# Pairs of batches share a tile of their last tokens, softmax sums on another engine, and a new order of work

## The chip, the cores and the metric

The kernel runs on one core of a Trainium2 chip. The core has a matrix engine (TensorE, PE in the profile, with its weight loads as PEld), a vector engine (VectorE, DVE), an engine for functions of one element (ScalarE, ACT), a programmable vector engine (GpSimd, POOL) and a sync engine (SyncE, SP), whose queue issues most transfers here. Each takes its instructions in the order in which the program lists them and waits where an instruction's input isn't ready. Matmuls write to PSUM, eight banks of 512 float32 for each of 128 partitions; everything else lies in SBUF. The metric is device time in microseconds, lower is better: the median of three runs.

## The reference, cut to what matters

Eight batches of 576 tokens, 8 heads of 64 channels. Keys and values are averaged over 8 neighbouring tokens, which leaves 72; ordinary softmax attention follows, and its output x (576 tokens by 512 channels) goes through a mixing block:

```
k_p, v_p = means of k, v over 8 tokens                  # 72 rows
attn = softmax(q @ k_p.T / 8)                           # 576 x 72 per head
x = attn @ v_p                                          # heads side by side: 576 x 512
theta = x @ w_theta
zr, zi = x * cos(theta), x * sin(theta)
y = w_tok_r @ zr + w_tok_i @ zi                         # over tokens, 576 x 576 each
u = x + y
out = u + max(u @ w_ch, 0)
```

All in float32. The three weights come as float64 and are turned into float32 pairs on the chip.

## The kernel before, in words

Products that need more than one pass's accuracy are split: a matrix a becomes a high part (`xh`, `zh`, `uh`, ...) and a remainder (`xl`, `zl`, `ul`), and a product is three matmuls, high by high, high by low, low by high.

The work is cut into streams, small generators that issue one step each time they are called. For each batch b:

- `k`, `v`, `Q`: loads (`load` L491, `queries` L580); `K`, `V`: the sums over 8 tokens (`pool` L518, `pool_sum` L476: three halving additions) and the layouts that attention needs (`keys` L560, `vals` L620).
- `S{b}.{m}` for five token tiles m (four of 128 tokens, the last of 64): scores, softmax (`soften` L680). Scores sit in PSUM tile `s`, two banks, of which there is one. For batches 0 and 1 (`SUMS_ON_ACT` = 2) ScalarE takes the maximum as its bias and does one exponential for each head, with the sum accumulated; for batches 2 to 7 VectorE subtracts the maximum, ScalarE does one exponential over all heads, and VectorE sums.
- `E`: for batches 2 to 7 the attention weights are transposed by VectorE and 16 small transfers (`turn` L840, for tiles 0 and 1, and for 2 to 4).
- `X{b}.{g}.{c}`: attention times values for one of four blocks of channels and for tokens 0 to 255 or 256 to 575 (`attend` L877). It writes x with channels on the partitions into `xT`, 640 columns wide: after 576 tokens the last 64 stand again (L906).
- `T{b}.{m}`: theta of one tile of 128 tokens (`rotate` L911): split x, 12 matmuls of 512 columns, then rounding to whole turns (L929, L931), 4 transposes of x, sine, absolute value, cosine, and the products with x, into `z`. Tile 4 holds the last 64 tokens twice; one sine gives cosines in one half and sines in the other (L957 to L963). So `z` has nine chunks of 128 rows.
- `Z{b}.{c}`: split of z for a block of channels (`take` L968). `M{b}.{c}.{hf}`: 27 matmuls with the token weights, for 256 or 320 tokens, added to x (`mix` L980), and the split of u.
- `F{b}.{c}.{hf}`: 12 matmuls with w_ch, maximum and sum (`final` L1015), a transposition by VectorE into `R`, and for each (b, c) four transfers to the output; those of the last batch go by halves, on two queues.

`h`, `w`, `W`, `c` are the streams of the weights, all within the first batches. The order is written out by hand as words in `SCHEDULE`: each word calls its stream once, and a last letter v, g or a says which engine (VectorE, GpSimd, ScalarE) does the step, where there is a choice. Each engine's queue is the order of the words:

```
for word in SCHEDULE.split():
    name, engine = (word[:-1], word[-1]) if word[-1] in "vga" else (word, None)
    now[0] = engine
    next(streams[name])
```

Of the kernel before, what the change touches and what calls it, by code (L numbers as in the profile page):

```python
# [9 lines left out]
F32 = mybir.dt.float32  # L10
# [20 lines left out]
D h1 k0.0 k0.1 K0.0 K0.1 K0.0a k0.2 w0.0 h0 K0.2 w0.0 Q0.0 w0.0v h0 w0.0g h1 h1v K0.2a K0.1v Q0.1 w0.0 K0 h2 Q0.0  # L31
h0g Q0.0v K0a K0 w1.0 Q0.2 K0a Q0.4 h0a h0 h0 Q0.1 Q0.1a h1v h0v S0.0 h0 w1.0 h1 S0.0 h0v Q0.3 h0 w1.0g h1 h2 S0.1
h2v S0.0 Q0.2 v0.0 S0.1 Q0.2v h2v h2 v0.1 Q0.4 h1g v0.2 k1.0 Q0.3 h2 w1.0v S0.0 h2v w0.1 S0.0 S0.1 h3 S0.2 Q0.4v
S0.0g Q0.3v S0.2 V0.0 w1.0 w0.0 S0.1 S0.2 S0.1 S0.0g S0.0 S0.3 w0.0v V0.1 S0.1g S0.3 S0.1g S0.0v V0.2 S0.2 S0.2 V0v
K1.0g S0.1 S0.3 V0 S0.3 S0.4 w0.1 S0.0 h1 S0.1v S0.2g S0.2g S0.0v k1.2 S0.1 S0.4 S0.1v X0.0.0 S0.3 h3 h1v X0.0.0v
S0.2 w0.1v X0.0.1 S0.4 w0.1v w0.1 h3a h2 X0.0.1v h3v S0.3v h3 w0.1 X0.0.3 w1.1 S0.3v S0.4 h3 k1.1 S0.2a w0.1v S0.4
S0.2 h3g S0.3 S0.3a S0.2a Q1.0 w2.0 h1 W0 w1.1 Q1.1 w1.1a h2v X0.0.3v S0.4g w3.0 S0.4g S0.3 h3 S0.3v h2 w2.0 W0a
X0.0.2 h3v X0.0.2v K1.1g w2.0a S0.4 S0.4a S0.4 Q1.0 S0.4v T0.0a w1.1a h3 Q1.1 w2.1 X0.2.3 w2.0a W0 w1.1 Q1.1a w1.0
W0 Q1.0a Q1.3 X0.2.3v w2.1 T0.0v w1.1 w3.1 w2.0 W0a W0 v1.0 Q1.2 w2.1a X0.2.1 K1 T0.0 w1.1v K1.2v w2.1a w1.0v w2.1
T0.0 X0.2.2 T0.0 W1 T0.1g w2.0 w2.0v T0.1v Q1.2 T0.0 T0.0 w3.0 X0.2.1v T0.0a X0.2.2v w3.0a V1.0v w3.0v X0.2.0 W1a  # L40
w2.1 Q1.3 T0.0 X0.2.0v T0.1 T0.3a W1 T0.3v w2.1g Q1.3a X0.2.3a T0.2a T0.1 W1 w3.1 w4.0 W1a w3.0 T0.0 T0.1 K1a T0.2g
w3.1v Q1.4 T0.2 T0.0 T0.2 W1 T0.1 v1.1 W2 T0.4g w3.1v T0.1 w4.0 T0.4v w3.0 w3.1 w3.0g w4.0a T0.1a T0.1 T0.2 W2v
T0.2 T0.2 W2 w4.0a T0.1 T0.3 W2 T0.2a W2a T0.1 T0.4 T0.2 w4.0 V1.1g c0 T0.3 w4.0 c0 w3.1 W2 T0.2 T0.2 w3.1g T0.4
T0.3 W3 c0g T0.4 T0.3 K1 T0.4 M0.0.0 T0.4 T0.3 W3a T0.4 T0.3a T0.3 T0.3 W3 T0.4 w4.0g c0 T0.3 c0 Q1.2a c0 Z0.0a W4
W4a c0v c1 Z0.0v W4 W4a c0a c0g W4 W4a V1g Q1.4 M0.0.0 M0.0.0 Z0.1a W4 K1v W4a c1 W4 W3 c1v W3a W3 c1 c1 M0.0.1
M0.0.0 c1 c1v Z0.1v c1a Z0.2a S1.0 c1g M0.1.1 S1.0 c2 Q1.4a Z0.2v c2 M0.0.1 c2v c2 c2 c2 k2.2 K2.2v c2v M0.1.0 S1.0
v1.2 S1.0 S1.0v S1.1 Z0.3a S1.0g S1.0 c3 M0.0.1g M0.1.0 S1.1 M0.1.1 V1.2g Z0.3v M0.2.0 V1v S1.0v c2a S1.1 S1.0 S1.0
S1.1 M0.3.0 M0.2.0 c2g S1.2 S1.0a c3 M0.2.0a V1 S1.0 c3v M0.0.0g S1.2 S1.1v M0.3.1 c3 S1.1v S1.2 c3 c3 M0.3.0
M0.0.0v S1.1 c3v M0.1.1v S1.1v S1.2 V1v V1v M0.0.1g M0.3.1 S1.1 S1.1 M0.2.1 Q2.0 S1.1a S1.1 X1.0.0 M0.1.1g c3a
S1.2v M0.3.1a S1.3 M0.2.1 c3g X1.0.0a M0.3.0a k2.0 S1.3 S1.2g S1.3 M0.3.1g M0.3.0g X1.0.1 M0.2.1g M0.2.1g S1.2  # L50
M0.1.0a X1.0.1v X1.0.2 F0.0.1 X1.0.2v K2.0v M0.2.0v X1.0.3 X1.0.3v S1.2a S1.4 M0.1.0v S1.3 T1.0a S1.2 S1.2 S1.2a
S1.3g S1.4 S1.3v F0.0.0 T1.0v F0.0.0 Q2.0 S1.2 S1.4 F0.0.1 k2.1 S1.3 S1.3a S1.4 F0.0.0 F0.0.1 T1.0 S1.3 v2.2 K2.1g
# [24 lines left out]
F2.0.1 X3.2.2v X3.2.3 T3.1v K5.2v F2.0.1 T3.1 S4.2 T3.0 S4.2 T3.0v T3.0 S4.3 T3.0 F2.0.1 S4.2g v5.0 T3.0 F2.1.1
# [53 lines left out]

EARLY, EXACT, V_ON_PE, K_ON_PE, Q_ON_PE, SUMS_ON_ACT = 2, 1, 1, 1, 2, 2


@with_exitstack
def tile_attn_moe(
# [52 lines left out]
    def pick():  # L191

        return now[0]
# [986 lines left out]
```

## Time and profile before

| | |
|---|---|
| runs | 614.71, 616.81, 618.32 us, median 616.81 |
| profiled execution: span, first to last instruction | 611.1 us; the page gives no other total for it |
| TensorE matmuls / weight loads busy | 590.0 / 548.7 us (97% / 90%) |
| VectorE, ScalarE, GpSimd busy | 475.6, 302.0, 331.4 us |
| granted TensorE clock, mean | 0.996 of full speed |
| chain that ended last | TensorE 60%, VectorE 18% of the span |

Busy time is the time in which an engine had at least one instruction under way. TensorE's matmuls overlap, so the mean of one is longer than the distance from one to the next; how fast matmuls really follow each other is read from the starts in a timeline, or from the chain.

### The profile page before, as it was taken

The numbers are of one execution on the slowest core, as the hardware profiler recorded it, in microseconds if no ns is written. First come the engines' busy times: TensorE is split into PE (matmuls) and PEld (weight loads), VectorE is DVE, ScalarE is ACT, GpSimd is POOL, SyncE is SP. The second block draws the span as 40 slices with busy tenths as digits, with TensorE's granted clock in tenths as the row PEclk, the third lists the DMA queues.
The fourth block names the chain that finished last, engine by engine and source line by source line (L and its number), as shares of the span: only waits on it lengthen the run. The fifth ranks groups of instructions, "written<-read, shape, count | busy, mean of one in ns | idle before, by whom it ended". The sixth has DMA issues, their size and how long they took to land.

```text
span 611.1 us, 11650 instructions
## 1 busy us (share of the span) xinstructions
PE 590.0 (97%) x4136; PEld 548.7 (90%) x4136; DVE 475.6 (78%) x933; ACT 302.0 (49%) x627; POOL 331.4 (54%) x492
## 2 busy tenths in 40 slices
PE   7899989998899999999999999999999999999997
PEld 6766889887799999999899999999999999998996
DVE  4999989889898978798978777898876875467425
ACT  3788858687743563236523652266334671515000
POOL 5561734356665778657867585337937644530130
PEclk9899999999999999999999999999999999999999
DMA  9978121368565646674527555624611331312115
GB/s 286 235 233 186 39 78 45 75 117 138 96 126 87 125 71 118 122 144 68 98 42 160 96 94 89 125 47 89 122 33 33 55 53 20 61 20 44 17 20 78
DMA packets 235386, 57.86 MB, mean 95 GB/s; under 512 B 223424, under 2 KB 223936, under 8 KB 235328
## 3 DMA queue, kind: packets, MB, share of 16 engines
q1 hardware_dynamic: 230464, 56.52, 46.1%
q10 hardware_dynamic: 4864, 0.59, 0.7%
q8 instruction: 33, 0.54, 0.4%
q14 instruction: 25, 0.20, 0.1%
HBM read 37.81 MB, written 9.44 MB: 77 GB/s over the span
## 4 chain that ended last, share of the span: by engine, by line
PE 60%; DVE 18%; DMA 5%; SPq 5%; POOL 4%; ACT 4%; issue 3%; DVEq 0%; POOLq 0%; ACTq 0%
PE py L996 31%; PE pf L1025 9%; PE pt L925 8%; PE pv L898 5%; PE s L707 3%; SPq L851 3%; DMA kpst<-in_k_dram 1%; DMA WTh_st<-in_moe_w_theta_dram 1%; DMA out_dram<-R 1%; PE px L935 1%; DVE xT L904 1%; SPq L587 1%; DVE zl L977 1%; DVE oT L1031 1%; DVE mx L741 1%
## 5 line engine op out<-in xcount | busy, mean ns | idle before, releaser
L996 PE MATMUL py<-WTh,zh 128*128 128x256 f32 (+1 forms) x576 | 86.7, 295 | 1.0 <-ACT zh L197 1.0
L996 PE MATMUL py<-WTh,zl 128*128 128x256 f32 (+1 forms) x576 | 87.1, 295 | 0.5 <-DVE oT L1031 0.5
L996 PE MATMUL py<-WTl,zh 128*128 128x256 f32 (+1 forms) x576 | 86.4, 293 | 0.0
L996 PEld LDWEIGHTS py<-WTh,zh 128*128 128x128 f32 x576 | 79.9, 188 | 1.6 <-ACT zh L197 1.4
L996 PEld LDWEIGHTS py<-WTh,zl 128*128 128x128 f32 x576 | 79.0, 188 | 1.0 <-DVE oT L1031 0.7
L996 PEld LDWEIGHTS py<-WTl,zh 128*128 128x128 f32 x576 | 79.7, 187 | 0.0
L1002 DVE TENSOR_TENSOR xT<-py,xT 128x256 f32<-128x256 f32 (+1 forms) x64 | 28.6, 447 | 41.4 <-PE py L996 41.3
L182 POOL TENSOR_TENSOR en<-e_eps,ri 128x256 f32<-128x256 f32 (+3 forms) x63 | 30.6, 505 | 42.9 <-DVE ri L766 32.6
L929 ACT ACTIVATE g<-pt,c_magic 128x512 f32<-128x512 f32 x38 | 26.1, 687 | 48.1 <-PE pt L925 28.1
L1025 PE MATMUL pf<-uh,chh 128*128 128x320 f32 (+1 forms) x256 | 46.4, 302 | 0.0
L925 PE MATMUL pt<-th,xh 128*128 128x512 f32 x160 | 45.1, 403 | 1.3 <-DVE xh L199 1.1
L1025 PE MATMUL pf<-ul,chh 128*128 128x320 f32 (+1 forms) x256 | 44.1, 293 | 0.0
L1025 PE MATMUL pf<-uh,chl 128*128 128x320 f32 (+1 forms) x256 | 44.1, 293 | 0.0
L925 PE MATMUL pt<-th,xl 128*128 128x512 f32 x160 | 43.2, 392 | 0.0
L925 PE MATMUL pt<-tl,xh 128*128 128x512 f32 x160 | 43.1, 391 | 0.0
L182 POOL TENSOR_TENSOR zl<-z,zh 128x256 fp32r<-128x256 f32 (+1 forms) x44 | 35.7, 843 | 10.9 <-ACT zh L197 10.6
L762 ACT ACTIVATE e_eps<-e_eps 128x576 f32<-128x576 f32 (+1 forms) x30 | 20.6, 686 | 42.4 <-DVE e_eps L758 42.2
L707 PE MATMUL s<-kpT,qT 128*128 128x144 f32 x256 | 38.5, 292 | 1.7 <-DVE tl L396 1.2
L977 DVE TENSOR_TENSOR zl<-z,zh 128x640 fp32r<-128x640 f32 (+1 forms) x42 | 33.2, 832 | 8.8 <-POOL zh L199 8.1
L1025 PEld LDWEIGHTS pf<-uh,chh 128*128 128x128 f32 x256 | 37.9, 188 | 1.5
L182 POOL TENSOR_TENSOR xl<-xT,xh 128x256 fp32r<-128x256 f32 x42 | 30.3, 744 | 15.8 <-DVE xh L199 9.3
L931 DVE SCALAR_TENSOR_TENSOR g<-g,pt 128x512 f32<-128x512 f32 x38 | 25.7, 677 | 15.6 <-ACT g L929 15.4
(250 smaller groups left out, 1448.2 us busy)
## 6 DMA issues: line engine op xcount, KB each, us to landing
out_dram<-R SPq DMA_DIRECT2D x112, 72.0 KB, 2.1
kpst<-in_k_dram SPq DMA_DIRECT2D x15, 512.0 KB, 4.4
vpst<-in_v_dram SPq DMA_DIRECT2D x28, 256.0 KB, 4.0
qsst<-in_q_dram SPq DMA_DIRECT2D x96, 72.0 KB, 2.7
eraw<-G SPq DMA_DIRECT2D x96, 60.0 KB, 2.2
eraw<-G SPq DMA_DIRECT2D x96, 40.0 KB, 2.0
WTh_st<-in_moe_w_theta_dram SPq DMA_DIRECT2D x4, 512.0 KB, 5.5
wcraw<-in_moe_w_ch_dram SPq DMA_DIRECT2D x4, 512.0 KB, 3.4
```

What stands on the lines that cost most here:

```text
L182: nc.gpsimd.tensor_tensor(out[:, r], a[:, r], b[:, r], op)
L707: nc.tensor.matmul(scs[c // 2][:n, 2 * SP * (c % 2) : 2 * SP * (c % 2 + 1)], qT[:, c, t0 : t0 + n], kpT[:, c, :], start=True, stop=True,)
L762: nc.scalar.activation(e[:n], e[:n], AF.Exp, scale=scale)
L851: nc.sync.dma_start(blocks(Ex, jj, i), blocks(Gx, i, jj))
L898: nc.tensor.matmul(pv[:, :gn], l, r, start=i == 0, stop=i == len(terms) - 1)
L925: nc.tensor.matmul(pt, l[:, c, :], r[:, c, :], start=i == 0, stop=i == 11)
L929: nc.scalar.activation(g, pt, AF.Identity, bias=c_magic)
L931: nc.vector.scalar_tensor_tensor(g, g, MAGIC, pt, ALU.subtract, ALU.subtract)
L977: ENG[pick()].tensor_tensor(zl[:, r], z[:, r, o], f32(zh[:, r]), ALU.subtract)
L996: nc.tensor.matmul(py[:, :n], l[:, kk, :], r[:, kk, t], start=i == 0, stop=i == 3 * NK - 1)
L1002: nc.vector.tensor_tensor(u, py[:, :n], u, ALU.add)
L1025: nc.tensor.matmul(pv[:, :n], l[:, kk, o], uhl[r][:, kk, t], start=i == 0, stop=i == 11)
```

## The change

- **Pairs.** Batches 2 and 3, 4 and 5, 6 and 7 share the tile of the last 64 tokens: 64 columns of one batch beside 64 of the other. Odd batches of a pair have no tile 4. Sine and cosine of the whole tile are taken, and four products with x put them into chunk 0 (for the even batch) and chunk 9 (for the odd) of a `z` that is now one tile with ten chunks. `weight_chunks` says which rows of the token weights belong to which chunk.
- **Softmax sums.** `SUMS_ON_ACT` is 8: all batches go the way of batches 0 and 1.
- **Pool sums.** Where VectorE sums over 8 tokens, one reduction takes the place of three additions.
- **x in two tiles**, `xa` (256 tokens) and `xb` (320), each twice. The final writes its result into x and not into a tile `oT`; the transposed result is a half, `R`, of which there are two, and it is written out by four transfers for each half.
- **Order.** Mix, theta and final issue their matmuls in three words each (9, 4 and 4 matmuls), `attend` uses a second bank for pairs, and all words stand in a new order with new engines.

```
-EARLY, EXACT, V_ON_PE, K_ON_PE, Q_ON_PE, SUMS_ON_ACT = 2, 1, 1, 1, 2, 2
+EARLY, EXACT, V_ON_PE, K_ON_PE, Q_ON_PE, SUMS_ON_ACT = 2, 1, 1, 1, 2, 8
...
+    def xpart(b, g0):
+        if (b, g0) not in xs:
+            tag, n = ("xb", PARTS[1][1]) if g0 else ("xa", PARTS[0][1])
+            xs[b, g0] = work([P, NC, n], F32, tag, f"{tag}{b}", bufs=2)
+        return xs[b, g0]
+
+    def paired(b):
+        return b >= EARLY
+
+    zflat = const([P, (NK + 1) * DM + 64], F32, "z")
+    z = zflat[:, 0 : (NK + 1) * DM].rearrange("p (a b) -> p a b", a=NK + 1)
+
+    def chunks(b):
+        return slice(1, NK + 1) if paired(b) and b % 2 else slice(0, NK)
+
+    def weight_chunks(b):
+        if paired(b) and b % 2:
+            return (0, 1, 2, 3, 5, 6, 7, 8, 4)
+        return (4, 0, 1, 2, 3, 5, 6, 7, 8)
...
     def pool_sum(t, width, dst, fine):
         w = width // 2
-        e = pick()
+        e = pick("vg")
+        if e == "v" and not fine:
+            x = t.rearrange("p c (r d) -> p c d r", d=D) if len(t.shape) == 3 else t.rearrange("p (r d) -> p d r", d=D)
+            nc.vector.tensor_reduce(dst, x, AX.X, ALU.add)
+            return
...
+            pv = bank([P, 512], "px" if paired(b) and c % 2 else "av", f"pv{b}_{g0}_{c}")
...
     (in theta, which rotate calls)
         for l, r in ((xh, th), (xh, tl), (xl, th)):
             for c in range(NC):
                 nc.tensor.matmul(pt, l[:, c, :], r[:, c, :], start=i == 0, stop=i == 11)
                 i += 1
-        yield
+            yield
...
+            x = work([P, NC, P], F32, "xe", f"xe{b}")
+            for j in range(2):
+                copy(pick("avg"), x[:, :, 64 * j : 64 * j + 64], xpart(b + j, 256)[:, :, 256:320])
+                yield
...
+            lo, hi = slice(0, 64), slice(64, 128)
+            for j, r in ((0, lo), (NK, hi)):
+                nc.vector.tensor_tensor(z[hi, j], px[r], s[r], ALU.mult)
+                yield
+                nc.vector.tensor_tensor(z[lo, j], px[r], g[r], ALU.mult)
+                yield
...
     (in mix)
-            for kk in range(NK):
+            for kk, kw in enumerate(weight_chunks(b)):
                 nc.tensor.matmul(
-                    py[:, :n], l[:, kk, :], r[:, kk, t], start=i == 0, stop=i == 3 * NK - 1
+                    py[:, :n], l[:, kk, :], r[:, kw, t], start=i == 0, stop=i == 3 * NK - 1
                 )
                 i += 1
-        yield
+            yield
...
     (in final)
-        oT = work([P, 320], F32, "oT", f"oT{b}_{c}_{hf}", bufs=2)[:, :n]
-        nc.vector.scalar_tensor_tensor(
-            oT, pv[:, :n], 0.0, xT[:, c, t], ALU.max, ALU.add
-        )
+        nc.vector.scalar_tensor_tensor(x, pv[:, :n], 0.0, x, ALU.max, ALU.add)
...
+            R = work([P, PARTS[1][1]], F32, "R", f"R{b}_{c}_{hf}", bufs=2)[:, :n]
+        nc.vector.transpose(R, x)
+        yield
         for i in range(4):
             ch0 = P * c + 32 * i
-            nc.sync.dma_start(
-                out[b, :, ch0 : ch0 + 32].rearrange("(x t) a -> t x a", t=32),
+            (nc.scalar if b == B - 1 and i % 2 else nc.sync).dma_start(
+                out[b, t, ch0 : ch0 + 32].rearrange("(x t) a -> t x a", t=32),
...
-        for m in range(5):
+        for m in range(4 if paired(b) and b % 2 else 5):
             stream(f"T{b}.{m}", rotate(b, m))
```

The new order begins `D k0.0 K0.0 Q0.0 k0.1 K0.0v`, where the old one began `D h1 k0.0 k0.1 K0.0`. The words around the start of the pair of batches 4 and 5, from the attention of the odd batch's second half to the first mix of the even one (the two copies and the split of x of tile T4.4 among them), are:

```
X5.2.3 X5.2.3v X5.2.0 X5.2.0v T4.3 Q6.0 F3.1.0 X5.2.1 X5.2.1v X5.2.2 X5.2.2v K6.0g F3.0.0 F3.0.0 T4.3 T4.3 T4.3a T4.4v
T4.4v S5.1 S5.0 T4.4v T4.4 T4.3 T4.3 S5.1g S5.1g T4.3 T4.4 S5.1 T4.4 F3.1.0 T4.4 T4.4 F3.0.0 F3.0.0 F3.3.1 F3.1.0
F3.1.0 T4.4 T4.4 k6.1 F3.3.0 T4.4a T4.4 T4.4 T4.4 F3.2.0 F3.2.0 F3.2.0 F3.2.0 F3.2.0 F3.2.1 F3.3.0 F3.3.0 K6.1g F3.3.0
K6 Z4.0a F3.1.0 M4.0.0 M4.0.0 Z4.0v M4.0.0
```

## Rows read from the trace of the kernel before

**Rows 1.** The page's first part: busy time of each engine, its share of the span, and instructions.
```profile
span 611.1 us, 11650 instructions
...
PE 590.0 (97%) x4136; PEld 548.7 (90%) x4136; DVE 475.6 (78%) x933; ACT 302.0 (49%) x627; POOL 331.4 (54%) x492
```

**Rows 2.** Busy time by stage: the stretch in microseconds, its length, and busy time (with instructions) of each engine, then TensorE's granted clock, the DMA engines' share and GB/s.
```profile
0.00:80.00 80.00, 72.57 (x464) 57.53 (x465) 68.43 (x135) 58.32 (x167) 40.30 (x60) 0.98 0.69 187
80.00:240.00 160.00, 151.55 (x1079) 141.69 (x1080) 136.55 (x265) 99.45 (x236) 94.76 (x148) 1.00 0.50 97
240.00:600.00 360.00, 359.26 (x2550) 343.06 (x2549) 265.39 (x524) 144.23 (x225) 196.34 (x285) 1.00 0.41 73
```

**Rows 3.** What TensorE waited for: in all, times, longest. The first and the last of 11 rows for 80 to 240 us, and the first of three for the time after it.
```profile
PE wt L434 <- DVE WTl L472: 1.6, 1, 1.6
...
PE s L707 <- DVE qT L592: 0.3, 1, 0.3
...
PE pv L898 <- POOL Vr L182: 0.4, 1, 0.4
```

**Rows 4.** The chain that ended last around 341 and 250 us, in order of time: start, length, what.
```profile
341.36 2.77 PE pt L925 x12
344.12 1.41 PE pf L1025 x12
345.54 0.44 PE px L935 x4
...
250.65 0.17 PE pkr L575
```

**Rows 5.** Groups of instructions by line, shapes kept apart, on TensorE and VectorE: line, engine, operation, output and input, shapes, count | busy us, mean ns of one | idle before, releaser.
```profile
L925 PE MATMUL pt<-th,xl 128*128 128x512 f32 x160 | 43.2, 392 | 0.0
...
L931 DVE SCALAR_TENSOR_TENSOR g<-g,pt 128x512 f32<-128x512 f32 x38 | 25.7, 677 | 15.6 <-ACT g L929 15.4
L741 DVE TENSOR_REDUCE mx<-s 128x8 f32<-128x576 f32 x30 | 22.4, 746 | 3.3 <-PE s L707 3.3
L954 DVE TENSOR_TENSOR z<-px,g 128x512 f32<-128x512 f32 x30 | 20.4, 680 | 4.1 <-ACT g L950 4.1
L758 DVE TENSOR_TENSOR e_eps<-s,mx 128x576 f32<-128x576 f32 x24 | 18.2, 758 | 4.4 <-POOL en L182 2.3 <-DVE mx L741 0.5
L764 DVE TENSOR_REDUCE sm<-e_eps 128x8 f32<-128x584 f32 x24 | 18.0, 748 | 3.2 <-ACT e_eps L762 3.2
L904 DVE TENSOR_SCALAR xT<-pv 128x320 f32<-128x320 f32 x26 | 12.4, 480 | 2.7 <-PE pv L898 2.7
L199 DVE CAST xh<-xT 128x512 fp32r<-128x512 f32 x7 | 3.5, 496 | 1.9 <-PE pt L925 1.6
L199 DVE COPY xT<-xT 128x256 f32<-128x256 f32 x2 | 0.7, 336 | 0.0
```

**Rows 6.** The same for ScalarE; behind the dots three lines of ScalarE's timeline (start, length) in a softmax of batch 1, and one piece of the chain that is no engine's work.
```profile
L929 ACT ACTIVATE g<-pt,c_magic 128x512 f32<-128x512 f32 x38 | 26.1, 687 | 48.1 <-PE pt L925 28.1 <-DVE z L954 15.1 <-DVE R L1044 4.8
L762 ACT ACT_TABLE_LOAD x17 | 21.8, 1283 | 6.8 <-DVE e_eps L758 6.6
L197 ACT CAST zh<-z 128x1152 fp32r<-128x1152 f32 x19 | 21.8, 1152 | 26.7 <-PE py L996 21.0 <-DVE z L962 4.7 <-DVE z L954 1.0
L950 ACT ACTIVATE g<-g,c_cos 128x512 f32<-128x512 f32 x30 | 21.7, 725 | 3.8 <-DVE g L948 3.1
L942 ACT ACTIVATE sn<-g 128x512 f32<-128x512 f32 x30 | 18.9, 632 | 17.3 <-DVE g L931 17.0
L762 ACT ACTIVATE e_eps<-e_eps 128x576 f32<-128x576 f32 x24 | 16.5, 686 | 30.7 <-DVE e_eps L758 30.6
...
117.83 0.21 ACT L746 ACTIVATE mx<-mx 128x8 f32<-128x8 f32 x1 [1.09 <-DVE mx L741]
118.12 0.32 ACT L750 ACTIVATE e_eps<-s,mx 128x72 f32<-128x72 f32 x1
...
120.69 0.30 ACT L754 ACTIVATE sm<-sm,c_eps 128x8 f32<-128x8 f32 x1
...
236.69 0.03 issue
```

**Rows 7.** The same groups for the sums over 8 tokens on VectorE.
```profile
L480 DVE TENSOR_TENSOR kpst<-kpst 128x512 f32<-128x512 f32 x3 | 2.1, 688 | 1.0 <-DMA kpst<-in_k_dram 1.0
L480 DVE TENSOR_TENSOR kpst<-kpst 128x256 f32<-128x256 f32 x3 | 1.3, 424 | 0.1
L485 DVE TENSOR_TENSOR kp<-kpst 128x128 f32<-128x128 f32 x3 | 0.9, 292 | 0.1
```

**Rows 8.** Issues of transfers on SP's queue (smallest, median and largest duration in ns, first and last start): the output, whole and by halves, and the attention's turn; then VectorE's wait for the output, and the time from issue to landing.
```profile
L1059 SPq DMA_DIRECT2D out_dram<-R x112: 315/506/1249, 137.4 to 585.9; - x112
L1049 SPq DMA_DIRECT2D out_dram<-rz x16: 315/410/714, 598.4 to 608.0; - x16
...
L851 SPq DMA_DIRECT2D eraw<-G x192: 591/624/1955, 155.2 to 527.6; - x192
...
  DVE R L1044: 4.2, 5
...
DMA to landing us min/median/max: 1.8/2.1/4.0
```

**Rows 9.** The last line of VectorE's timeline: start, length.
```profile
607.16 0.45 DVE L1044 STREAM_TRANSPOSE rz<-oT 128x256 f32<-128x256 f32 x1
```

More of the change, by code (lines that the diff above doesn't have):

```diff
@@ L36 @@
[L36 to L40, printed above, removed]
@@ L189, in tile_attn_moe, with pick @@
     now = [None]
-    def pick():
+    def pick(engines):
         return now[0]
@@ L878, in attend @@
         g0, tiles, gn = group(m)
[L879 to L880 removed]
         eh, ev, er = parts[b, g0]
[L882 removed]
+        x, Vr = xpart(b, g0), Vrs[b]
         if b == 0 and g0:
@@ L932, in rotate, with absolute @@
         yield
+        angles[b, m] = g
+    angles = {}
+    def absolute(out, g):
+        if pick("av") == "a":
+            nc.scalar.activation(out, g, AF.Abs)
+        else:
+            nc.vector.tensor_scalar(
+                out.bitcast(I32), g.bitcast(I32), 0x7FFFFFFF, None, ALU.bitwise_and
+            )
+    def rotate(b, m):
+        if m < 4:
+            g0 = 0 if m < 2 else 256
+            o = slice(P * m - g0, P * m - g0 + P)
+            x = xpart(b, g0)[:, :, o]
+        elif not paired(b):
+            x = ends[b]
+        else:
+            x = work([P, NC, P], F32, "xe", f"xe{b}")
+            for j in range(2):
+                copy(pick("avg"), x[:, :, 64 * j : 64 * j + 64], xpart(b + j, 256)[:, :, 256:320])
+                yield
+        xh = work([P, NC, P], F32R, "xh", f"xh{b}_{m}", bufs=2)
+        xl = work([P, NC, P], F32R, "xl", f"xl{b}_{m}", bufs=2)
+        copy(pick("avg"), xh, x)
+        yield
+        ENG[pick("vg")].tensor_tensor(xl, x, f32(xh), ALU.subtract)
+        yield
+        yield from theta(b, m, xh, xl)
+        g = angles[b, m]
+        other = b == 0 and m % 2
         px = bank([P, DM], "mm" if other else "px", f"px{b}_{m}", bufs=2 if other else 1)
         for c in range(NC):
-            nc.tensor.transpose(px[:, P * c : P * c + P], xT[:, c, o], ident)
+            nc.tensor.transpose(px[:, P * c : P * c + P], x[:, c], ident)
         yield
         s = temp(b, m, "sn", DM)
-        if b not in zs:
-            zs[b] = work([P, NK, DM], F32, "z", f"z{b}")
-        z = zs[b]
-        if m < 4:
+        if m < 4 or paired(b):
             nc.scalar.activation(s, g, AF.Sin, scale=-TWO_PI)
             yield
-            if pick() == "a":
-                nc.scalar.activation(g, g, AF.Abs)
-            else:
-                gi = g.bitcast(I32)
-                nc.vector.tensor_scalar(gi, gi, 0x7FFFFFFF, None, ALU.bitwise_and)
+            absolute(g, g)
             yield
```

377 lines of the change are left out of this document (190 added, 187 removed).

## The prediction, made before the changed kernel ran

> **What bounds the kernel now.** I read the page's busy row first, then the busy times by stage, then what TensorE waited for, then the chain. TensorE is busy 97% of the span, VectorE 78%, ScalarE 49%, GpSimd 54% [rows 1]. A single mean hides two regimes. From 240 to 600 us TensorE is busy 359.26 of 360 us, while VectorE has 265.4 and ScalarE 144.2: here the time is what TensorE has to do. Before 80 us VectorE is busy 68.4 of 80 and TensorE idles for 7.4; from 80 to 240 us TensorE idles for 8.45 of 160 [rows 2]. Its waits in that stretch are 11 rows with 8.7 us together, none over 1.6; after 240 us they are three rows with 0.8 us [rows 3]. So an edit shortens the run if it takes instructions from TensorE, or idle time from the first 240 us; work moved between the other engines pays only if TensorE waits less or more by it.
>
> In the stretch from 80 to 240 us the two rows of TensorE differ: 151.6 us busy with matmuls, but 141.7 with weight loads, that is 8.45 us free by one and 18.3 by the other [rows 2]. The Trainium skill (Perfetto Trace Analysis, Identifying the Most-Contended Engine) says that matmul busy time is a poor measure of headroom and the share of weight loads a good one. By that rule this stretch holds 18.3 us and not 8.45, and the first rival below is the case in which it is right.
>
> **Part by part.**
>
> *Shared last tile.* Batches 2 to 7 form three pairs, and of each pair one theta tile goes: 12 matmuls and 4 transposes. In the chain 12 such matmuls take 2.77 us and the 4 transposes 0.44 [rows 4]. Three tiles are 3 x 3.21 = 9.6 us, all in the stretch where TensorE never waits. The 27 matmuls of each mix stay 27. I take -9.6 us, and see no reason for another value: these instructions are gone and their place is filled.
>
> *The wait that this adds.* The shared tile can't start before the second half of the pair's odd batch has passed attention, and all mixes of the even batch need it. In the new order nothing else stands between. From the third group of its theta matmuls the way to the first mix is one matmul's latency 0.39, g 0.69, rounding 0.68, sine 0.63, Abs taken as a sine's 0.63, cosine 0.73, a multiply 0.68, the zh copy 1.15: 5.6 us, 5.8 with six handovers of the 0.03 us that the chain calls issue [rows 5, 6]. What TensorE is given meanwhile is counted in the new order. Batch 4: nine groups of four final matmuls at 1.41/3 = 0.47, the transposes 0.44, the keys' four the same, together 5.1; batch 2: the same and one more at 0.17, 5.3; batch 6: five groups, the transposes and one theta tile, 5.6 [rows 4]. Short by 0.7, 0.5 and 0.2. Ahead of the tile, from the last attention to its first theta matmul: 0.39 for a matmul, taken as theta's, + 0.48 for the evacuation + 0.34 copy + 0.50 xh = 1.7 us, against 1.4 us of TensorE's work in batches 4 and 6 [rows 5]: another 0.6 in all. I take +2.0 us. The lower end is 0 (the chain fits if engines come early), the upper end 3 x 5.8 = 17 us, with no cover at all. What is queued behind the waiting mix on TensorE is everything: it runs in order.
>
> *Softmax sums on ScalarE.* For 30 tiles (batches 2 to 7) VectorE loses the subtraction and the sum: 30 x (0.758 + 0.748) = 45 us [rows 5]. ScalarE does eight exponentials with accumulated sums for one of 0.686. Of batch 1's tile they run from 118.12 to 120.69 (next instruction), with a 0.21 multiply before and 0.30 after: 3.1 us, +2.4 a tile, 72 us in all [rows 6]. In the order of words the switches between exponential and sine fall from 38 to 28, each a load of 1.28: -13 us. ScalarE goes from 302 to about 361 us and VectorE to about 430: neither is near TensorE's 580. Direct cost 0, hidden by TensorE's work; the bank of scores, held longer, is a rival below.
>
> *Pool sums by one instruction.* VectorE's three adds take 0.69 + 0.42 + 0.29 = 1.40 us for 1024 elements. The trace has no such strided reduction; by the sum over 584 elements in 0.748 it would take 1.31, and I take that. If the stride doubles it, 2.6. In the new order VectorE does 24 of these sums for batches 1 to 7, where it did 11, and GpSimd loses 13 [rows 7]. Even so VectorE would have 24 x 2.6 = 62 us of these in place of 11 x 1.4 = 15, and at some 480 us would still be under TensorE. I take 0 for the end, between -2 and +3.
>
> *x in two tiles, output by halves.* The final writes into x, so the same two VectorE instructions per final remain. Output transfers of batches 0 to 6 double from 112 to 224. A whole one takes SP 0.506 us to issue, the last batch's half ones 0.410: 224 x 0.41 - 112 x 0.506 = +35 us on SP's queue. Behind them there stand the 16 issues of each attention turn, 0.62 each, and the loads of k, v and q; what waits for those is the attention, 13 to 28 us of TensorE's work later. Also each half sits in one of two R buffers: 4 x 0.41 + 2.1 to land is 3.8 us, so two in 3.8, and a final takes TensorE 1.4 to 1.8. VectorE waited 4.2 us for R before [rows 8]. I take 0 for TensorE, since VectorE has 45 us back; upper end +8.
>
> *New order.* Matmul groups of mix, theta and final are issued as three words each, so other work can go between. After 240 us there is nothing to win. Before the first mix the sums of VectorE's and ScalarE's work in the words ahead of it are the same within 3% and 9%: no change, with +-5 us as ends, since loads now come in another order. From 80 to 240 us I let half of the 8.7 us of waits go [rows 3]: -4.3, between 0 and 11.3: a stretch whose weight loads are as dense as after 240 us, 343.06/360 = 95.3%, would have done the 141.7 us in 148.7 [rows 2]. The tail, VectorE's last 0.45 us until 607.6 and 3.5 more for the last transfer, stays [rows 9].
>
> **Sum.** -9.6 + 2.0 - 4.3 = -11.9 us. Span 611.1 to 599.2. The median of the runs, 616.81, lies 5.7 above the span, which the change does not touch: 604.9 us.
>
> **Rivals.**
>
> 1. *More than that.* Finer groups fill all of the early stretch: -9.6 + 2.0 - 11.3 = -18.9, 597.9; with 5 us won at the start, 593. For it: the gap between the two rows of TensorE. Against it: VectorE is busy 136.6 of 160 us there [rows 2], and that is work which mostly stays (batches 0 and 1 had their sums on ScalarE already). The rule of the skill cited above speaks for this rival.
>
> 2. *Given back.* The pair's chain finds no cover at a place or two: with +9.6 (a little over half of 17) and no early gain the run stays at 616.8. For it: the shared tile has many steps on three engines, in which any queue in front adds. Against it: three places only.
>
> 3. *Slower: the bank of scores.* One pair of banks serves all score groups. Before it was free after the maximum and the subtraction, 0.75 + 0.76 = 1.5 us; now after the maximum, 0.21 and the exponentials, 0.75 + 0.21 + 2.57 = 3.5 [rows 5, 6]. The next score group stands in TensorE's line and everything behind it waits. In the new order the work between two score groups of batches 2 to 7 is mostly 5 to 13 us, but in nine of the gaps under 5.6 and in three 4.0. It decides where the exponentials start over 0.5 us late: behind a zh copy (1.15) or a table load (1.28) [rows 6]. If all nine lose these 2.43 us, that is 22 us: 627. It turns the result once the nine lose 1.7 us each (15 us). Against it: ScalarE is under 60% busy, and the order has most score groups together, so that loads are rare.
>
> That a tile is not shared is no case of its own: the loop over tiles ends at 4 for odd batches.
>
> **How the numbers follow.** The forecast (600 to 612, by its own terms) has 0.56, the first rival 0.22, the second 0.13, the third 0.09. 0.5% is 3.1 us, about what a measurement here can tell from no change: faster means under 613.7, slower over 619.9. Forecast and first rival are faster, with a little of the second: 0.79. Same 0.12, slower 0.09. The range reaches into the first rival to 592 and into the second to 616, which leaves 0.07 below and 0.13 above.
>
> **What would show it.** Theta matmuls drop from 480 to 444, transposes from 160 to 148. VectorE's busy time falls by some 40 us, ScalarE's rises by some 60, with 27 to 29 table loads. If the pair's wait matters, the waits list py on ACT or GpSimd zh near the first mixes of batches 2, 4 and 6, over 1 us each; if rival 3 holds, s on ACT e_eps. TensorE's idle time after 240 us over 5 us, or a span above 608, makes the prediction wrong; a span under 592 makes the early stretch mis-sized.

## The result and the profile after

The changed kernel takes 623.71 us (median; 622.14 to 626.19), the kernel before 617.47 beside it: ratio 1.0113, 95% interval [1.0081, 1.0146]. The forecast of 604.9 was wrong in direction, and 623.71 lies above the range, 592 to 616. Below, ratios are to the kernel before, run on the same chip beside the kernel in question; a gain against the changed kernel is the difference from 1.0113, times 616 us, good to some 3 us, since each ratio has an interval of its own.

The changed kernel's page, first part, and its busy time by stage (as [rows 1] and [rows 2]):

```profile
span 622.4 us, 12089 instructions
...
PE 591.1 (95%) x4088; PEld 542.5 (87%) x4088; DVE 458.3 (74%) x835; ACT 360.3 (58%) x1141; POOL 325.1 (52%) x455
```

```profile
0.00:80.00 80.00, 71.01 (x448) 54.18 (x448) 69.41 (x123) 60.39 (x172) 33.46 (x51) 1.00 0.69 189
80.00:240.00 160.00, 150.89 (x1040) 138.29 (x1039) 133.67 (x241) 110.28 (x393) 97.70 (x145) 0.99 0.50 97
240.00:600.00 360.00, 351.08 (x2471) 332.09 (x2469) 245.13 (x453) 189.17 (x577) 191.13 (x255) 1.00 0.39 72
```

The 48 instructions of TensorE are gone (4136 to 4088), worth 9.6 us by the prediction's rows. Yet TensorE is busy 591.1 us, 1.1 more than before, so its remaining work took 10.7 us longer; and its idle time rose from 21.1 (611.1 - 590.0) to 31.3, by 10.2. -9.6 + 10.7 + 10.2 = 11.3, the whole growth of the span. In every execution with both on record the time is 1.7 to 2.0 us above the span, so the profiled one of the kernel before, with its 611.1, took some 613 us where the median is 617.47, and about 4 of the 11.3 us are the choice of this execution. Most of the added idle time is where I saw nothing to lose: after 240 us TensorE stands 8.9 of 360 us, before it was 0.7 [rows 2]. Its waits there (in all, times, longest; the first three of nine, and the fifth), and then VectorE's own over the whole run:

```profile
PE pv L940 <- DVE xb L946: 2.8, 1, 2.8
PE pf L1100 <- DVE xb L1105: 1.5, 1, 1.5
PE pv L940 <- DVE eraw L916: 1.3, 1, 1.3
...
PE py L1072 <- ACT zh L213: 0.7, 2, 0.4
```

```profile
DVE ri L810 <- ACT sm L798: 23.2, 14, 3.6
...
DVE R L1111 <- DMA out_dram<-R: 12.7, 9, 3.1
```

TensorE waits for VectorE's evacuations, not for the pair's `zh`. VectorE is busy for fewer microseconds than before and is late all the same: it stands 23.2 us at the reciprocal until ScalarE has the sums, and everything queued behind stands with it. The groups of the pool sums (line, engine, operation, out and in, shapes, count | busy us, mean ns | idle before):

```profile
L521 DVE TENSOR_REDUCE kp<-kpst 128x128 f32<-128x1024 f32 x8 | 15.7, 1963 | 1.0 <-DMA kpst<-in_k_dram 1.0
L521 DVE TENSOR_REDUCE vp<-vpst 128x128 f32<-128x1024 f32 x6 | 12.0, 2007 | 0.9 <-DMA vpst<-in_v_dram 0.9
L521 DVE TENSOR_REDUCE kpr<-kprst 64x64 f32<-64x512 f32 x5 | 5.4, 1078 | 1.3 <-DMA kprst<-in_k_dram 1.3
```

A reduction over 1024 elements takes 1.98 us, not the 1.31 that I estimated. Next the place where TensorE loses most: VectorE's and GpSimd's timelines (start, length), TensorE's, and TensorE's windows:

```profile
360.32 3.59 DVE L215 CAST er<-eraw 32x320 fp32r<-32x320 f32 x4
363.94 2.23 DVE L909 TENSOR_TENSOR er<-eraw,er 32x320 fp32r<-32x320 f32 x2
366.20 0.49 DVE L1105 SCALAR_TENSOR_TENSOR xb<-pf,xb 128x320 f32<-128x320 f32 x1
...
368.34 1.05 DVE L521 TENSOR_REDUCE vpr<-vprst 64x64 f32<-64x512 f32 x1
...
372.86 0.89 DVE L946 TENSOR_SCALAR xb<-pv 128x320 f32<-128x320 f32 x2
```

```profile
360.75 1.35 POOL L215 CAST eh<-eraw 128x1280 fp32r<-128x1280 f32 x1 [2.83 <-DMA eraw<-G]
362.17 3.14 POOL L198 TENSOR_TENSOR eraw<-eraw,eh 128x640 fp32r<-128x640 f32 x2
```

```profile
366.75 0.85 PE L1100 MATMUL pf<-uh,chh 128*128 128x320 f32 x4 [1.48 <-DVE xb L1105]
...
373.41 0.41 PE L940 MATMUL pv<-eh,Vh 128*128 128x320 f32 x1 [2.76 <-DVE xb L946]
...
374.83 1.06 PE L1100 MATMUL pf<-uh,chh 128*128 128x256 f32 x4
375.69 1.05 PE L1100 MATMUL pf<-uh,chl 128*128 128x256 f32 x4
```

```profile
370.00:374.00 4.00, 1.24 (x9) 1.03 (x9) 3.86 (x8) 2.28 (x15) 2.77 (x4) 1.00 0.78 127
374.00:378.00 4.00, 4.00 (x20) 3.90 (x19) 3.39 (x9) 3.87 (x9) 0.69 (x1) 0.57 0.69 98
```

The tiles belong to the attention weights of batch 5 behind their turn: `eraw` as they land and later their remainder, `eh` the high part for 64 of the 72 averaged rows, `er` both parts for the other 8. VectorE's six small instructions on `er` last 5.8 us beside GpSimd's work on `eraw` and `eh`. The final's evacuation (366.20) and attention's (372.86) come late behind them, and TensorE stands 1.48 and 2.76 us. After the second stall its granted clock is 0.57 over four microseconds, most of them at the lower level of 1.2 GHz: four matmuls of a final take 0.86 (374.83 to 375.69), where a third of a final's 1.41 [rows 4] is 0.47. So this stall costs again after it has ended: 4 x (1 - 0.57) = 1.7 us, and 4 x (1 - 0.59) = 1.6 us behind the one at 128 us that is shown at the end. These 3.3 us are the part of the 10.7 that I can name (the kernel before loses 1.6 us in the same way, from 14 to 20 us); no run isolates the rest.

### The profile page after: what moved, and what is told of

Its sections match the earlier page's. It is cut to its first block, busy times and chain, and to the rows that moved or that the text cites. A ratio compares the mean times of both kernels' runs of the same rounds, so it can differ in the third digit from the quotient of the medians.

```text
span 622.4 us, 12089 instructions
## 1 busy us (share of the span) xinstructions
PE 591.1 (95%) x4088; PEld 542.5 (87%) x4088; DVE 458.3 (74%) x835; ACT 360.3 (58%) x1141; POOL 325.1 (52%) x455
## 5 line engine op out<-in xcount | busy, mean ns | idle before, releaser
L794 ACT ACTIVATE e_eps<-s,mx 128x72 f32<-128x72 f32 (+1 forms) x304 | 92.7, 329 | 4.5 <-DVE en L820 1.3
L1072 PE MATMUL py<-WTh,zl 128*128 128x320 f32 (+1 forms) x576 | 85.9, 296 | 0.9 <-DVE xb L1078 0.8
L794 ACT ACTIVATION_READ_ACCUMULATOR e_eps<-s,mx 128x1 f32 (+1 forms) x304 | 65.2, 214 | 0.0
L198 POOL TENSOR_TENSOR zl<-z,zh 128x384 fp32r<-128x384 f32 (+1 forms) x64 | 51.0, 830 | 26.6 <-ACT zh L213 15.3
L1100 PE MATMUL pf<-uh,chh 128*128 128x256 f32 (+1 forms) x256 | 47.0, 306 | 2.7 <-DVE xb L1105 2.4
L1100 PE MATMUL pf<-uh,chl 128*128 128x256 f32 (+1 forms) x256 | 45.2, 299 | 0.0
L1100 PE MATMUL pf<-ul,chh 128*128 128x256 f32 (+1 forms) x256 | 43.9, 295 | 0.0
L1100 PEld LDWEIGHTS pf<-uh,chh 128*128 128x128 f32 x256 | 38.3, 192 | 5.0 <-DVE xb L1105 3.2
L1100 PEld LDWEIGHTS pf<-uh,chl 128*128 128x128 f32 x256 | 38.3, 192 | 0.2
L790 ACT ACTIVATE mx<-mx 128x8 f32<-128x8 f32 (+1 forms) x40 | 8.2, 206 | 51.1 <-DVE mx L785 50.9
L751 PEld LDWEIGHTS s<-kpT,qT 128*128 128x128 f32 x256 | 33.9, 189 | 4.3 <-DVE qT L215 1.4
```

What stands on the lines that cost most here:

```text
L198: nc.gpsimd.tensor_tensor(out[:, r], a[:, r], b[:, r], op)
L751: nc.tensor.matmul(scs[c // 2][:n, 2 * SP * (c % 2) : 2 * SP * (c % 2 + 1)], qT[:, c, t0 : t0 + n], kpT[:, c, :], start=True, stop=True,)
L790: nc.scalar.mul(mx[:n], mx[:n], -scale)
L794: nc.scalar.activation(e[:n, x], scs[j][:n, SP * y : SP * y + SP], AF.Exp, bias=mx[:n, x : x + 1], scale=scale, accum_out=sm[:n, x : x + 1],)
L1072: nc.tensor.matmul(py[:, :n], l[:, kk, :], r[:, kw, t], start=i == 0, stop=i == 3 * NK - 1)
L1100: nc.tensor.matmul(pv[:, :n], l[:, kk, o], uhl[r][:, kk, t], start=i == 0, stop=i == 11)
```

## The experiments

The theories: **A**, ScalarE's sums make VectorE or the score bank late; **B**, the long strided pool reductions do; **C**, the new order as a whole bunches the work, and something is late anyhow; **D**, VectorE and GpSimd lengthen each other's work, and the order sets such pairs where VectorE is late; **E**, the pair's chain.

### Parts undone, and a part alone

The softmax of batches 2 to 7 as before; in this order a tile's subtraction then can overwrite exponentials that the tile ahead still needs, so other numbers are computed by the same instructions:

```
-SUMS_ON_ACT = 8
+SUMS_ON_ACT = 2
```

> The changed kernel with the softmax of batches 2 to 7 as before: VectorE subtracts the maximum and sums, ScalarE does one exponential per tile. Theory A (the sums on ScalarE are the cause: VectorE, whose queue is in order, stands 23 us at the reciprocal until ScalarE has the sums, and is late elsewhere): at least 6 of the lost us come back, 617 us or less, the reciprocal's wait falls under 6 us, and TensorE idles under 5 us after 240 us. Theory B (the strided pool reductions are the cause): VectorE gets 45 us more of work on top of the reductions, so the time stays at 622 or rises to some 628. Theory C (the new order and the pairing): within 3 us of 623.7.

The pool sums as three adds again:

```
-        if e == "v" and not fine:
+        if False:
```

> The changed kernel with the pool sums as three adds again where VectorE does them (24 sums of 1.40 us for 24 of 1.98, some 14 us of VectorE less, stall by stall 0.6 us). Theory A: within 2 us of 623.7, since VectorE goes on standing at the reciprocal. Theory B: at least 5 us come back, 618.5 or less, and the waits of TensorE for the finals' and attention's evacuations after 240 us fall by half. Theory C: within 3 us of 623.7.

Both:

> Both parts undone, with shared tile, half outputs and the new order kept. Theory A and theory B: 605 to 615 us, as forecast for the rest, with TensorE idle after 240 us under 3 us. Theory C (order and pairing): 619 or more, with TensorE still idle for over 6 us after 240 us, at the starts of the pairs.

And in the kernel before the softmax part alone (`SUMS_ON_ACT` 2 to 8):

> The kernel before with the softmax part of the change alone: sums on ScalarE in all batches, old order. Theory A: the wait at the reciprocal appears here too (15 us or more) and the run loses 6 us or more, 623 or over. Theory B and theory C: within 3 us of 617.5. My forecast's step (no direct cost) says the same.

Measured: 638.92 us without the softmax part (ratio 1.0366 [1.0328, 1.0404]), 627.56 with adds (1.0195 [1.0151, 1.0238]), 639.58 with both undone (1.0393 [1.0348, 1.0438]), and 660.19 for the softmax part in the old order (1.0716 [1.0678, 1.0753]). Each part undone makes the new order slower. No theory's numbers fit the first two (B had let the first rise to 628). For both undone only theory C's bound is met, 619 or more with over 6 us of idle time after 240 us: TensorE is busy 346.55 of 360 us there, 13.5 idle. With the softmax as before VectorE has 40 us more to do (498.6 busy); with the adds only 4 more (462.1), and their rows below say why it isn't less. And the softmax part alone costs the old order 44 us, on theory A's side of that forecast. There, what TensorE waited for and VectorE's wait:

```profile
PE s L707 <- ACT e_eps L750: 15.3, 8, 5.2
PE s L699 <- ACT e_eps L750: 12.0, 5, 4.6
```

```profile
DVE ri L766 <- ACT sm L754: 46.2, 22, 3.7
```

That is my third rival, the held bank of scores, with 27.3 us of TensorE's time, in an order that doesn't space the score groups; in the new order this wait is 0.8 us once after 240 us. What the parts cost within the new order can't be read from undoing them in it. The adds' rows in the changed order show a second thing:

```profile
L524 DVE TENSOR_TENSOR kpst<-kpst 128x512 f32<-128x512 f32 x8 | 5.8, 727 | 1.1 <-DMA kpst<-in_k_dram 1.1
L524 DVE TENSOR_TENSOR vpst<-vpst 128x512 f32<-128x512 f32 x6 | 5.6, 930 | 1.2 <-DMA vpst<-in_v_dram 1.2
```

Three adds take 0.73 + 0.53 + 0.47 = 1.73 us for keys and 0.93 + 0.72 + 0.58 = 2.24 for values, not the 1.40 of [rows 7]: beside GpSimd they are lengthened as the `er` copies are. The last of the three takes 0.29 us in each instance in which GpSimd is idle and 0.42 to 0.99 beside it. A reduction of the changed kernel takes 1.89 to 2.00 us without GpSimd and 1.89 to 2.04 beside it. So adds in place of reductions take no work off VectorE in this order, and this run can't price the reductions.

### One relief at a time, order kept

Two words of the order to other engines:

```
-E5.2g E5.2v k6.0 E5.2v E5.2g
+E5.2g E5.2a k6.0 E5.2g E5.2g
```

> The changed kernel with two words of its order given to other engines: the copies of batch 5's last er tile go from VectorE to ScalarE and the subtraction behind them to GpSimd. At 360 us these six instructions take VectorE 5.8 us beside GpSimd's work on the same tile, where 2.2 us would do by their shortest rows, and TensorE then stands 1.5 and 2.8 us and runs at a lower granted clock behind it. Theory D (VectorE and GpSimd lengthen each other where both read and write SBUF, and the order puts such pairs where VectorE is late): both stalls go, 4 to 6 us come back, 617.5 to 620. Theory C (the bunched order as a whole): VectorE is late there anyhow, under 2 us come back.

Fewer exponentials, with `if b < 2:` ahead of the eight with their sums:

```
+            else:
+                for j in range(2):
+                    nc.scalar.activation(
+                        e[:n, 4 * j : 4 * j + 4],
+                        scs[j][:n, 0 : 4 * SP].rearrange("p (x g) -> p x g", g=SP),
+                        AF.Exp, scale=scale,
+                    )
+                nc.scalar.activation(sm[:n], mx[:n], AF.Identity, bias=c_eps[:n])
```

> The changed kernel in its order, with two exponentials per tile in place of eight with their sums for batches 2 to 7; the maximum isn't used and the sums are left out (the maximum's tile is copied in their place). ScalarE loses some 65 us, VectorE gains nothing. Theory A (ScalarE's sums make VectorE and the score bank late): 6 us or more come back, 617.5 or less, and VectorE's wait at the reciprocal falls from 23 us under 8. Theories C and D: under 3 us, since TensorE's stalls end with VectorE and not with the sums.

The shared tile without its wait:

```
-xpart(b + j, 256)[:, :, 256:320]
+xpart(b, 256)[:, :, 256:320]
```

> The changed kernel, but the shared theta tile takes both halves from the even batch, so that it no longer waits for the odd batch's attention (the odd batch's last 64 tokens are then computed from other data). My forecast's step (2.0 us for the three pairs' chain): 2 us come back. Theory E (the pair's chain is where the time went): 5 us or more, 618.7 or less. Theories A, C and D: within 1.5 us, since TensorE hardly waits for zh in the changed kernel.

Reductions over neighbouring elements:

```
-t.rearrange("p c (r d) -> p c d r", d=D)
+t.rearrange("p c (d r) -> p c d r", d=D)
```

> The changed kernel with its pool reductions over neighbouring elements instead of every 64th (so other sums, by one changed view). By 1.28 ns per element of the sum over 584 elements one takes 1.3 us instead of 1.98 if the stride is what costs, and still 1.98 if it is not. Theory B (slow reductions make VectorE late): 3 us or more come back, 620.7 or less. Theories A, C and D: under 2 us.

Measured: the `er` words 617.93 us (1.0031 [1.0001, 1.0061]), a gain of 5.1 us from two letters; two exponentials 620.03 (1.0064 [1.0035, 1.0093]), 3.0 us, with the reciprocal's wait down from 23.2 to 2.8; neighbouring elements 615.30 (0.9996 [0.9962, 1.0030]), 7.2 us; the shared tile without its wait 624.17 (1.0129 [1.0083, 1.0175]), nothing. D and B hold with their numbers and E falls. A's is half met: 3.0 us, good to 2.7, is the edge of what C and D allowed. The reciprocal's wait with two exponentials, and the reduction over neighbours, 1.20 us:

```profile
DVE ri L819 <- ACT sm L807: 2.8, 3, 1.4
...
L521 DVE TENSOR_REDUCE kp<-kpst 128x128 f32<-128x1024 f32 x8 | 9.6, 1197 | 1.0 <-DMA kpst<-in_k_dram 1.0
```

Whether the `er` words cost by contention or as plain load, one letter tells:

```
-E5.2g E5.2v k6.0 E5.2v E5.2g
+E5.2a E5.2v k6.0 E5.2v E5.2g
```

> The changed kernel with one word of its order changed: the rounding copy of batch 5's last eh tile goes from GpSimd to ScalarE, so that nothing of GpSimd's stands beside VectorE's four er copies at 360 us. VectorE keeps all its six instructions there. Theory D, contention: the copies fall from 3.6 to about 1.4 us, and half or more of the 6 us that moving all six off VectorE gave comes back, 618 to 621. Rival, plain load (VectorE simply has six instructions too many there): under 1.5 us come back, since VectorE has the same list.

Measured: 621.00 us (1.0074 [1.0048, 1.0100]), a gain of 2.4. VectorE's and GpSimd's timelines of that run:

```profile
360.70 1.35 DVE L215 CAST er<-eraw 32x320 fp32r<-32x320 f32 x4
362.09 2.25 DVE L909 TENSOR_TENSOR er<-eraw,er 32x320 fp32r<-32x320 f32 x2
```

```profile
362.42 3.33 POOL L198 TENSOR_TENSOR eraw<-eraw,eh 128x640 fp32r<-128x640 f32 x2 [4.10 <-ACT eh L213]
```

With GpSimd idle the same four copies take 1.35 us in place of 3.59; the subtraction, now beside GpSimd, still takes 2.25. So the contention is shown. Its share of the 5.1 us is not: the gain of 2.4 is good to 2.6 only, and it is a net one. TensorE's two stalls for VectorE there, 1.48 and 2.76 us, are gone, and in their place it stands once, for ScalarE, which does the `eh` copy (1.26 us) ahead of the exponentials:

```profile
PE s L751 <- ACT e_eps L794: 2.9, 1, 2.9
```

In the run with both words moved this wait is 1.3 us. With the 1.7 us of low clock, the traces give 1.5 + 2.8 + 1.7 - 2.9 = 3.1 us back here and 6.0 - 1.3 = 4.7 with both words, near the measured 2.4 and 5.1: what sets the two runs apart is ScalarE's wait. Whether VectorE's six instructions would still be too many there if ScalarE were on time, the rival of plain load, stays open.

### All reliefs together, and a part alone in the old order

The edits of the `er` words, of the fewer exponentials and of the neighbouring elements in one kernel:

> Three reliefs together in the changed order: the words of batch 5's er tile off VectorE, two exponentials per tile without maximum and sums in batches 2 to 7, and pool reductions over neighbouring elements (sums and pools left out or other, as in the single runs). One by one they gave 6, 4 and 8 us. If VectorE and ScalarE being late is the whole of what my forecast missed, they add up to some 15 to 18 us and the time is 606 to 609, near the 604.9 of the forecast. Theory C (the bunched order): they overlap and 612 or more remains.

And the pool part alone in the kernel before:

```
+        if e == "v" and not fine:
+            x = t.rearrange("p c (r d) -> p c d r", d=D) if len(t.shape) == 3 else t.rearrange("p (r d) -> p d r", d=D)
+            nc.vector.tensor_reduce(dst, x, AX.X, ALU.add)
+            return
```

> The kernel before with the pool part of the change alone: where VectorE has a pool sum, one strided reduction in place of three adds (11 sums, 1.98 for 1.40 us by the shortest rows of both), old order. Theory B (reductions as such make VectorE late): 2 us or more are lost, 618 or over. Theories C and D: within 2 us of 616, since a reduction doesn't lengthen beside GpSimd (1.96 us with and without it) and the adds do (0.69 free, up to 1.81 beside it).

Measured: 605.82 us (0.9838 [0.9805, 0.9872]) and 616.58 (0.9987 [0.9967, 1.0008]). The single gains sum to 5.1 + 3.0 + 7.2 = 15.3, together they gave 17.0. The relieved kernel's page and stages:

```profile
PE 584.3 (97%) x4088; PEld 540.3 (90%) x4088; DVE 437.8 (73%) x829; ACT 304.0 (50%) x725; POOL 324.6 (54%) x457
```

```profile
80.00:240.00 160.00, 154.62 (x1090) 143.44 (x1090) 132.30 (x250) 94.86 (x258) 98.96 (x146) 1.00 0.52 100
240.00:600.00 360.00, 357.72 (x2544) 341.23 (x2542) 239.29 (x453) 146.81 (x290) 191.44 (x260) 1.00 0.40 74
```

It leaves work out and is no kernel to use; but it is close to the one that I had priced, with reductions near 1.31 us and a softmax that costs nothing, and it lands within 1 us of the forecast (by its ratio 10 us below the kernel before, where the forecast had 11.9). Of the 18.8 us between forecast and measurement the three reliefs account for 17.0, good to 3. Theory C, as a cause of its own, falls: shared tile, half outputs and new order together can stand as forecast, though no run takes one of them alone. In the old order, where reductions are few (11 sums, not 24), they cost nothing measurable.

### What it acts through, with the computation kept

The `er` words stay off VectorE in all that follow. One sum later in the order:

```
-S1.3v K2.2v S1.3 S1.3 K2.0v S1.4 S1.4 S1.4v
+S1.3v K2.2v S1.3 S1.3 S1.4 S1.4 S1.4v K2.0v
```

> The changed kernel, all of its arithmetic kept, with batch 5's er words off VectorE and one pool sum of batch 2 moved in the order behind the reciprocal and multiplication of batch 1's last score tile: in the changed kernel VectorE takes this sum (1.9 us) ahead of them at 124 us, and TensorE stands 2.2 us for the multiplication's result, then runs at a granted clock of 0.91. Theory D with B: another 2 to 4 us beyond the 6 of the er words, 614 to 616. Theory C: no more than the er words gave, 617 to 618.

ScalarE's last softmax instruction left out, the added 1e-9 (the sums are at least 1, so that in float32 it changes nothing):

```
-            nc.scalar.activation(sm[:n], sm[:n], AF.Identity, bias=c_eps[:n])
```

> The changed kernel with the er words off VectorE (617.9 us so far), and ScalarE's last instruction of each softmax tile left out: it adds 1e-9 to sums of at least 1. It takes 0.30 us and stands between the exponentials and VectorE's reciprocal. Theory A (VectorE standing at the reciprocal for ScalarE is a cause by itself): its 23.7 us of waits fall by about 15 x 0.3 = 4 to 5 us, and 1 to 2 us of time come back. Theory B (the reductions alone are what is left): under 0.7 us.

Half of each large sum on GpSimd:

```
+            if len(t.shape) == 3:
+                nc.vector.tensor_reduce(
+                    dst[:, 0], t[:, 0].rearrange("p (r d) -> p d r", d=D), AX.X, ALU.add
+                )
+                t, dst, e = t[:, 1], dst[:, 1], "g"
...
```

> The changed kernel with the er words off VectorE, and of each pool sum of VectorE over 1024 elements one half reduced by VectorE and the other added by GpSimd (14 sums: VectorE loses 14 us, GpSimd gains some 22). Theory B (the 2 us blocks in VectorE's queue make it late): most of the 8 us that the contiguous reduction gave comes back here too, 611 to 614. Theory D (what GpSimd does beside VectorE costs as much as it frees): 617 or over, with longer VectorE instructions of SBUF to SBUF.

Three sums later, and `K2 K2v` behind them:

```
-S1.3v K2.2v S1.3 S1.3 K2.0v S1.4
+S1.3v S1.3 S1.3 S1.4
-S1.4a S1.4 X1.2.2 X1.2.2a
+S1.4a S1.4 K2.2v K2.0v X1.2.2 X1.2.2a
-T1.1v K2 K2v X1.2.1a X1.2.0 F0.1.0 X1.2.0a X1.2.3 M0.2.1a
+T1.1v X1.2.1a X1.2.0 F0.1.0 X1.2.0a X1.2.3 K2 K2v M0.2.1a
-T4.1 V6.1v T4.1 T4.1 T4.3v
+T4.1 T4.1 T4.1 T4.3v
-E5.2g E5.2a k6.0
+E5.2g E5.2a V6.1v k6.0
```

> The changed kernel with the er words off VectorE and three pool reductions later in the order: batch 2's last key sums behind all of batch 1's softmax, one of batch 6 from 349 us to behind the er words. No instruction is added or taken away. Theory B: VectorE's list is too long only where such a block stands ahead of what TensorE needs next, so the stalls at 127 us (2.0) and 362 us (1.3) go and 2 to 4 us come back, 614 to 616. Theory C: they come up elsewhere, 617 to 618.

The last softmax instruction left out, the split and the three moves together:

> All four together, with the arithmetic kept but for the added 1e-9: er words off VectorE, no last instruction of the softmax on ScalarE, half of each large pool sum on GpSimd, three reductions later. If they add up as the three reliefs did, 6 + 1.5 + 5 + 3 us come back, 608 us, and the run is faster than both kernels; if GpSimd takes back what VectorE gets, 614 to 618.

Measured: 618.97 (1.0039 [1.0014, 1.0064]), no gain over the `er` words; 616.90 without the last instruction (0.9996 [0.9970, 1.0023]), 2.2 us better than the `er` words alone, with the reciprocal's wait at 19.8 instead of 23.7; 622.29 split (1.0058 [1.0022, 1.0095]), 1.7 us worse; 624.88 with the moves (1.0148 [1.0109, 1.0188]), 7.2 us worse; 629.29 for all (1.0211 [1.0182, 1.0240]). The 2.2 and the 1.7 are within their noise of 2.5 and 2.9 us: that the wait at the reciprocal is a cost by itself is likely by this run and the one with two exponentials, and not shown. A block that is put later makes something else late, as theory C said of both moves, and worse than it said: this order has no room for one. Of the single sum it is the tile's next multiplication: TensorE's one stall of 2.0 us there became two, of 0.9 and 1.6. With the three moves it is the keys and queries; TensorE's first wait of that run:

```profile
PE s L751 <- DVE qT L636: 2.9, 2, 2.7
```

The split's profiled execution (624.29 us) loses before 80 us: there GpSimd's part of a key sum, from 41.51 to 43.17 us, stands ahead of the last multiplication of a softmax of batch 0, and TensorE waits 1.1 us for it. From 46 to 59 us TensorE then has about half its clock (0.65 over 44 to 50, 0.53 over 50 to 60), which costs 6 x 0.35 + 10 x 0.47 = 6.8 us, more than the split loses. That the wait brought the clock down is not shown, nor that the split costs anything without it:

```profile
50.00:60.00 10.00, 10.00 (x34) 6.90 (x34) 6.31 (x10) 5.57 (x9) 4.75 (x7) 0.53 0.42 106
```

So I gave words to an engine that was idle at that place instead of moving them. First, of the version without the last instruction:

```
-S1.3 S1.3 K2.0v S1.4
+S1.3 S1.3 K2.0g S1.4
```

> The last version (er words off VectorE, no last softmax instruction, 616.9 us) with one more word given away: batch 2's pool sum that stands ahead of batch 1's last multiplication in VectorE's line goes to GpSimd, which is idle from 126.7 to 134 us there. VectorE gets 1.9 us where TensorE stands 2.2 us for it. Theory B (place and length of such a block): 2 to 3 us come back, 614 to 615. Theory C: under 1 us, something else is late next.

Then batch 5's `er` copies too:

```
-E5.2g E5.2a k6.0 E5.2g E5.2g
+E5.2g E5.2g k6.0 E5.2v E5.2g
```

> The same, and batch 5's four er copies on GpSimd instead of ScalarE, the subtraction behind them again on VectorE. ScalarE then has 1.9 us less ahead of the exponentials for which TensorE stands 1.2 us at 364 us (the score bank). Score bank decides there: another 1 to 2 us, 612 to 614. If GpSimd's eight instructions in a row make the odd batch's attention wait for eraw instead: no gain or a loss of 1 to 2.

Measured: 613.98 us (0.9975 [0.9955, 0.9994]), 1.3 us better by the ratios, within their noise of 2.0, and below the kernel before by a quarter of a per cent, just clear of noise: the one version with the results kept that is faster than both kernels. And 615.84 (1.0008 [0.9985, 1.0031]): the score bank's wait of 1.3 us goes, and in its place TensorE again stands for VectorE:

```profile
PE pv L939 <- DVE xb L945: 2.1, 1, 2.1
```

## Why the prediction was wrong, step by step

- *Shared tile, -9.6*: the count is right. Theta matmuls are 3 x 148 = 444, transposes 148. The price was not measured alone; with the reliefs the whole run comes out as forecast.
- *The wait that this adds, +2.0*: 0, its lower end. TensorE waits 0.7 us for ScalarE's `zh` after 240 us, and taking the wait away gained nothing.
- *Softmax sums, 0*: **the first step that failed**: "Direct cost 0, hidden by TensorE's work". ScalarE's busy time (360.3 for "about 361") and its 28 table loads came as worked out; but I compared busy totals with TensorE's, and asked what waits for the score bank, not what is queued behind VectorE's reciprocal, which now waits for ScalarE in every tile. Price: 3.0 us in the new order, barely clear of its noise, and 44 in the old.
- *Pool sums, "I take 0 for the end, between -2 and +3"*: **the term that failed most**: the gain from a shorter reduction is 7.2 us. The stride costs 1.98 / 1.20 = 1.65 times. The 1.98 us lie half way between the 1.31 that I took and the 2.6 that I named, so the size was in my sight; I priced both at 0 because VectorE's total stays under TensorE's. A 2 us block in an in-order queue delays what stands behind it; which of TensorE's waits the 7.2 us are was not isolated. VectorE fell by 17 us, not some 40: the 40 left out that the 24 reductions take 38.3 us where the adds took 15.5.
- *Half outputs, 0*: VectorE's wait for `R` rose from 4.2 [rows 8] to 12.7 us. No run took this alone away; since the relieved kernel still has 8.9 of it and lands on the forecast, little of it should reach the end.
- *New order, -4.3, and "After 240 us there is nothing to win"*: there was something to lose. From 80 to 240 us TensorE idles 9.1 us, where 8.45 were before; the early gain came only with the reliefs (5.4). The stretch without idle time showed that the old order was fitted to the old durations, not that it has slack. For the new order's pairs of VectorE and GpSimd instructions (5.1 us at 360 us) I had no term. Two signs that I had named for being wrong are there: 8.9 us of idle time after 240 us where 5 were the limit, and a span of 622.4 where it was 608.
- *Span to time, +5.7*: only 1.7 to 2.0 us lie between span and time. It does not hurt the forecast, which is in effect 11.9 us below the median.
- *Rivals.* The third was the right mechanism in the wrong order of work. The one that won, VectorE late with less to do, wasn't on the list.

The Trainium skill (SBUF — State Buffer, Who interferes with whom) says that VectorE's copies in a two-port mode and its instructions with two SBUF inputs contend with GpSimd for one pair of ports, and its reductions do not. The runs agree: four `er` copies 3.59 us beside GpSimd and 1.35 without, while a reduction takes 1.89 to 2.04 us beside it and 1.89 to 2.00 without. It would have warned of the `er` words, and it spoke for the reductions against the adds.

## What to carry to other kernels

An order of work tuned to the last microsecond is a set of due times: a longer or waiting instruction on an engine with a quarter of its time free still costs, where it stands ahead of an evacuation. So price an edit by what stands behind it in its engine's line at the tightest places, not by busy totals. And when a change moves work and order together, relieve one cost at a time inside the new order: undoing parts in an order made for them told nothing of their price.

## What the runs showed of the hardware

- VectorE's sum of 8 elements that lie 64 apart: 1.98 us for 1024 elements, 1.20 when they are neighbours.
- Four VectorE copies of 32x320 from SBUF to SBUF: 1.35 us alone, 3.59 beside GpSimd.
- Not every TensorE stall lowers the granted clock: after one of 1.97 us, in the run with the `er` words moved, it was 1.00 over the next 8 us. After one of 2.76 us in the changed kernel it was 0.57 over the next 4 us, and after one of 2.20 us, at 128 us, 0.59:

```profile
124.00:128.00 4.00, 1.80 (x9) 1.13 (x7) 3.90 (x6) 1.72 (x9) 0.74 (x2) 1.00 0.43 68
128.00:132.00 4.00, 4.00 (x16) 3.02 (x17) 2.91 (x10) 0.81 (x4) 0.07 (x1) 0.59 0.53 131
```
